# Batch 0 of an attention and GLU kernel: folded norm products, inverses ahead of the score copies, one exp per column block

**Chip, cores, metric.** The kernel runs on one core of one Trainium2 chip. The metric is the device time of one execution in microseconds (us), given as the median of several executions. Experiments 1 and 2 ran on one chip, 3 to 5 on a second and 6 on a third, each with the kernel before beside them (829.74, 829.61 and 829.73 us), so small differences of time are compared only within one of these calls. TensorE does the matrix products, VectorE and ScalarE the work on single elements (the exps and sigmoids on ScalarE), and the DMA engines the loads.

## The reference, cut to what matters

```python
# q, k, v: (4, 6016, 256); tau = 1; w_gate, w_val: (256, 1536); w_out: (1536, 256)
qn = q / (np.linalg.norm(q, axis=1, keepdims=True) + 1e-06)     # a norm per column, over the 6016 rows
kn = k / (np.linalg.norm(k, axis=1, keepdims=True) + 1e-06)
s = kn.transpose(0, 2, 1) @ qn / tau                            # 256 x 256 scores per batch
a = np.exp(s - s.max(-1, keepdims=True))
a /= a.sum(-1, keepdims=True) + 1e-09
x = (v @ a).reshape(24064, 256)
gate = 1.0 / (1.0 + np.exp(-(x @ w_gate)))
return gate * (x @ w_val) @ w_out
```

The scores of a batch need all of its rows of q and k. So batch 0 begins with a stretch in which 12 MB of rows are loaded while TensorE can do no more than follow them. Only then can the dense part (the GLU of all rows) begin. It takes nearly all of the time. While it runs for one batch, the scores of the next are made beside it.

## The kernel before: the parts that matter

The loads stand in one queue, in this order: all q and k rows of batch 0 but the first group, the first rows of v, and the six weight tiles (gate and value in turn).

```python
    for t0, nt in groups0[2:]:
        load_qk(0, t0, nt)
    load_v(0, 0)
    ...
    for fg in range(NFG):
        for w, src in enumerate((moe_w_gate, moe_w_val)):
            nc.gpsimd.dma_start(out=w_sb[w][fg], in_=...)
    load_v(0, 1)
```

The squares of the rows are added up on VectorE. What is not added up goes to TensorE on its own, as "norm products" (a product with a column of ones, `ps_n`). After the last scores follow the norm products, the square root, the inverses, the spreading of the key norms over the partitions (`ps_rk`), and the exps:

```python
    for n, (sq, nt) in enumerate(parts):           # parts: the sum, the eleventh group, two short groups
        norm_mms(ps_n0, sq, nt, n == 0, n == len(parts) - 1, (1, 0) if n else (0, 1))
    st[0]["n"] = ps_n0
    norms_sqrt(0)
    nc.scalar.preload_act_table(ACT.Exp)
    copy_s(0, 0)
    norms_inv(0)
    copy_s(0, 1)
    busy(3)                                        # filler products of no use
    spread_k(0, 0, pso, "o")
    spread_k(0, 1, pso, "o")
    busy(1)
    weights(0, 0)                                  # two multiplications and two exps each
    weights(0, 1)
    ... # transposes of the first v rows
    sums(0, 0)
    gh(0, 0, psg, "g", act=False)
    gh(0, 1, psv, "v", act=True)
    sums(0, 1, pss, "s")
    gh(0, 2, psg, "g", act=False)
    gh(0, 3, psv, "v", act=True)
    nc.scalar.preload_act_table(ACT.Sigmoid)
    gh(0, 4, pso, "o", act=False)
```

`gh` multiplies the 256 x 256 attention weights (`e_sb`) with one tile of a GLU weight. This gives `ps_gh` in a bank of PSUM, the memory that takes TensorE's results, and VectorE or ScalarE evicts it (copies it out) to `gh_G` or `gh_H`. There are twelve such products. I number them from the first: the first needs the first gate weights, the second the first value weights. The fifth and the following share two banks (`pso`), and from the sixth on they stand between the first dense GLU products.

Of the kernel before, what the change touches and what calls it, by code (L numbers as in the profile page):

```python
# [9 lines left out]
FP32 = mybir.dt.float32  # L10
BF16 = mybir.dt.bfloat16
ACT = mybir.ActivationFunctionType
ALU = mybir.AluOpType
# [4 lines left out]
def kernel(  # L18
# [20 lines left out]
    nc = tc.nc  # L39
    P = nc.NUM_PARTITIONS  # L40
# [7 lines left out]
    NT = N // P  # L48
    CB = C // P
# [3 lines left out]
    TPC = 4  # L53
# [12 lines left out]
    def pool(name, bufs, **kw):  # L66
        return ctx.enter_context(tc.tile_pool(name=name, bufs=bufs, **kw))
# [4 lines left out]
    attp = pool("attp", 1)  # L72
# [14 lines left out]
    def mm(out, lhsT, rhs, start, stop, **kw):  # L87
        nc.tensor.matmul(out, lhsT=lhsT, rhs=rhs, start=start, stop=stop, **kw)  # L88
# [21 lines left out]
    t0, nt = groups0[0]  # L110
# [15 lines left out]
    shift = consts.tile([P, 1], FP32)  # L126
# [10 lines left out]
    for fg in range(NFG):  # L137
        for w, src in enumerate((moe_w_gate, moe_w_val)):
            nc.gpsimd.dma_start(
                out=w_sb[w][fg],  # L140
                in_=src.rearrange("(t p) f -> p t f", p=P)[:, :, ds(fg * FG, FG)],
# [11 lines left out]
    def score(b, t0, u):  # L153
        q_sb, k_sb = qk[b, t0]
        if t0 == 0 and u == 0:
            st.setdefault(b, {})["s"] = pss.tile([P, CB, C], FP32, tag="s", name="ps_s")
        ps_s = st[b]["s"]
        t = t0 + u
        for j in range(CB):
            mm(  # L160
                ps_s[:, j, :],
                q_sb[:, u, ds(j * P, P)],
                k_sb[:, u, :],
                start=(t == 0 and j == 0),
                stop=(t == NT - 1),
                skip_group_check=True,
            )

    def squares(b, t0, nt, which, engine, sq=None):
        src = qk[b, t0][which]  # L170
        if sq is None:
            sq = sqpool.tile([P, TPC, C], BF16, tag=f"sq{which}", name=f"sq{which}")
        if engine is nc.scalar:
            nc.scalar.activation(out=sq[:, :nt, :], in_=src[:, :nt, :], func=ACT.Square)  # L174
        else:
            engine.tensor_tensor(  # L176
                out=sq[:, :nt, :], in0=src[:, :nt, :], in1=src[:, :nt, :], op=ALU.mult
            )
        return sq

    def norm_mms(ps, sqs, nt, first, last, order=(0, 1)):

        for w in order:
            sq = sqs[w]
            for u in range(nt):
                for j in range(CB):
                    mm(
                        ps[:, w * CB + j : w * CB + j + 1],
                        sq[:, u, ds(j * P, P)],
                        ones_bf[:, 0:1],  # L190
                        start=(first and w == order[0] and u == 0 and j == 0),
                        stop=(last and u == nt - 1),
                        skip_group_check=True,
                    )

    def acc_start(b):
        st.setdefault(b, {})["acc"] = [
            attp.tile([P, TPC, C], BF16, tag=f"acc{w}", name=f"acc{w}") for w in range(2)
        ]
# [75 lines left out]
    def norms_sqrt(b):  # L275
        s = st[b]
        s["r"] = attp.tile([P, 2 * CB], FP32, tag="r", name="r")
        nc.scalar.activation(out=s["r"], in_=s["n"], func=ACT.Sqrt)

    def norms_inv(b):  # L280
        r = st[b]["r"]
        nc.vector.tensor_scalar(out=r, in0=r, scalar1=1e-6, scalar2=None, op0=ALU.add)
        nc.vector.reciprocal(r, r)
        if inv_tau != 1.0:
            nc.vector.tensor_scalar(
                out=r[:, :CB], in0=r[:, :CB], scalar1=inv_tau, scalar2=None, op0=ALU.mult
            )
# [8 lines left out]
    def copy_s(b, j):  # L296
        s = st[b]
        if j == 0:
            s["x"] = attp.tile([P, CB, C], FP32, tag="x", name="x_sb")
        nc.vector.tensor_copy(out=s["x"][:, j, :], in_=s["s"][:, j, :])  # L300

    def weights(b, i):

        s = st[b]
        e = attp.tile([P, CB, P], BF16, tag=f"e{i}", name=f"e_sb{i}", bufs=2)
        for j in range(CB):
            y = attp.tile([P, P], FP32, tag=f"y{i}{j}", name="y_sb")
            nc.vector.tensor_tensor(
                out=y, in0=s["x"][:, j, ds(i * P, P)], in1=s["rk"][i], op=ALU.mult
            )  # L310
            nc.scalar.activation(  # L311
                out=e[:, j, :], in_=y, func=ACT.Exp, bias=shift, scale=s["r"][:, j : j + 1]
            )
        s.setdefault("e", []).append(e)
        s.setdefault("rrow", [])

# [152 lines left out]
    def busy(n):  # L469

        ps = psg.tile([P, CH], FP32, tag="g", name="ps_busy")
        for _ in range(n):
            mm(ps, ones_bf, ones_wide, True, True)

    ps_n0 = psm.tile([P, 2 * CB], FP32, tag="m", name="ps_n")

    n_acc = NT // TPC - 1
    acc_start(0)
    acc = st[0]["acc"]
    last0 = len(groups0) - 1  # L480
    parts = [(acc, TPC)]
    for g, (t0, nt) in enumerate(groups0):
        engines = (nc.vector, nc.scalar) if g < last0 else (nc.scalar, nc.vector)
        sq = [squares(0, t0, nt, w, engines[w], acc[w] if g == 0 else None) for w in range(2)]
        if 0 < g < n_acc:
            for w in range(2):
                nc.vector.tensor_tensor(out=acc[w], in0=acc[w], in1=sq[w], op=ALU.add)  # L487
        elif g:
            parts.append((sq, nt))
        for u in range(nt):  # L490
            score(0, t0, u)
        if n_acc - 3 <= g <= n_acc:
            busy(1)

    for n, (sq, nt) in enumerate(parts):
        norm_mms(ps_n0, sq, nt, n == 0, n == len(parts) - 1, (1, 0) if n else (0, 1))
    st[0]["n"] = ps_n0
    norms_sqrt(0)
    nc.scalar.preload_act_table(ACT.Exp)
    copy_s(0, 0)  # L500
    norms_inv(0)
    copy_s(0, 1)
    busy(3)
    spread_k(0, 0, pso, "o")
    spread_k(0, 1, pso, "o")
    busy(1)
    weights(0, 0)
    weights(0, 1)
    late = []
    transpose_v(  # L510
# [123 lines left out]
```

## Time and profile before

| before | us |
|---|---|
| median of 3 runs (range) | 829.78 (829.66 to 829.87) |
| span of the profiled execution | 827.8 |
| last key rows landed | 32.86 |
| first / second `ps_gh` | 36.92 / 37.35 |
| eighth `ps_gh` | 42.82 |

The page says that TensorE is busy 98% of the time. That is an average over a start in which it is not the bound and a dense part in which it is. Such a change is read from the start alone: what waits there, and for what. The timeline lists instructions in order of time (start, us, engine, line, operation, output and input, shape, count; in brackets the idle time just before and what ended it). These lines of the kernel before, besides those which the prediction shows, matter later:

```profile
33.52 0.84 PE L88 MATMUL ps_n<-ones_bf,sq 128*128 128x1 bf16 x28
...
39.60 1.28 ACT L521 ACT_TABLE_LOAD   x1
...
42.08 0.69 ACT L377 ACTIVATE gh_H<-ps_gh,rrow 128x512 bf16<-128x512 f32 x1
...
42.14 0.74 DVE L379 TENSOR_SCALAR gh_G<-ps_gh,rrow 128x512 bf16<-128x512 f32 x1
...
42.82 0.59 PE L88 MATMUL ps_gh<-w_val,e_sb 128*128 128x512 bf16 x2
```

The first line is the tail of the norm products, to 34.36. The last three belong together. The eighth `ps_gh` starts 0.05 after ScalarE's eviction ends (42.08 + 0.69 = 42.77), while VectorE's still runs, to 42.88.

### The profile page before, as it was taken

To read this page: it belongs to the slowest core of one execution; us is meant where nothing else is said; L and a number is where in the kernel's file an instruction comes from. 1 tells how busy PE (TensorE), PEld (TensorE's weight loads), DVE (VectorE), ACT (ScalarE), POOL (GpSimd) and SP (SyncE) were. 2 spreads that over 40 slices of the span, in tenths; PEclk is the share of its full clock that TensorE was granted. 3 is DMA by queue.
4 is the path that set the end of the run, shared out by engine and by line. 5 is a ranking of instruction groups with operands and counts; after the bars stand their busy time and mean duration, and the time that the engine had idled before them with its cause. 6 is when DMAs were issued, how large, how long until landed. Compare 5 with 4: busy or idle time off the path is not lost.

```text
span 827.8 us, 13658 instructions
## 1 busy us (share of the span) xinstructions
PE 810.3 (98%) x5138; PEld 500.3 (60%) x5150; DVE 590.4 (71%) x1025; ACT 391.7 (47%) x644; POOL 83.4 (10%) x159
## 2 busy tenths in 40 slices
PE   4899999999999999999999999999999999999998
PEld 3556666665665666665575666666566566666566
DVE  6677877787667777778767777777766666666665
ACT  4654444446644444445654444444655444444442
POOL 5532100002210100000211010000000000000000
PEclk8799999999999999999999999999999999999999
DMA  9999633226746433223876452223322423322111
GB/s 208 207 205 213 108 52 90 58 55 136 159 85 120 97 87 61 55 52 85 156 141 127 81 101 62 51 62 77 64 60 63 73 52 85 69 49 69 47 36 71
DMA packets 79026, 77.17 MB, mean 93 GB/s; under 512 B 50800, under 2 KB 55920, under 8 KB 78960
## 3 DMA queue, kind: packets, MB, share of 16 engines
q0 software_dynamic: 23920, 38.81, 28.3%
q1 hardware_dynamic: 54752, 36.91, 17.5%
q8 instruction: 40, 0.66, 0.3%
q10 hardware_dynamic: 288, 0.59, 0.2%
q14 instruction: 26, 0.21, 0.1%
HBM read 78.64 MB, written 24.64 MB: 125 GB/s over the span
## 4 chain that ended last, share of the span: by engine, by line
PE 95%; DMA 3%; POOL 1%; DVE 1%; issue 0%; ACT 0%; POOLq 0%
PE ps_o L88 30%; PE ps_gate L88 29%; PE ps_val L88 29%; PE ps_s L88 4%; DMA k_sb<-in_k_dram 3%; PE ps_gh L88 2%; DVE hT L424 0%; POOL q_sb L97 0%; PE ps_n L88 0%; POOL k_sb L97 0%; DVE sq L176 0%; PE ps_end L88 0%; ACT g_sb L423 0%; ACT e_sb L311 0%; PE ps_busy L88 0%
## 5 line engine op out<-in xcount | busy, mean ns | idle before, releaser
L424 DVE TENSOR_TENSOR hT<-ps_val,g_sb 128x512 bf16<-128x512 f32 (+1 forms) x576 | 391.2, 680 | 205.2 <-ACT g_sb L423 200.7
L423 ACT ACTIVATE g_sb<-ps_gate 128x512 bf16<-128x512 f32 (+1 forms) x576 | 338.3, 588 | 385.9 <-PE ps_gate L88 379.6
L88 PE MATMUL ps_gate<-vT,gh_G 128*128 128x512 bf16 (+1 forms) x1152 | 337.6, 375 | 0.2
L88 PE MATMUL ps_val<-vT,gh_H 128*128 128x512 bf16 (+1 forms) x1152 | 337.5, 375 | 0.3
L88 PE MATMUL ps_o<-w_out_sb,hT 128*128 128x256 bf16 x2244 | 324.9, 273 | 0.0
L88 PEld LDWEIGHTS <-hT 128*128 128x128 bf16 x2268 | 221.0, 98 | 124.6
L88 PEld LDWEIGHTS <-gh_H 128*128 128x128 bf16 x1152 | 112.7, 98 | 131.6 <-issue 1.0
L88 PEld LDWEIGHTS <-gh_G 128*128 128x128 bf16 x1152 | 112.4, 98 | 37.8 <-DVE gh_G L379 0.5
L106 POOL DMA_DIRECT2D v_sb<-in_v_dram x48 | 25.6, 533 | 620.5 <-DMA vT<-v_sb 487.5
L450 DVE COPY out_sb<-ps_o 128x256 f32<-128x256 f32 x187 | 77.4, 414 | 12.6 <-PE ps_o L88 12.6
L88 PE MATMUL ps_s<-k_sb,q_sb 128*128 128x256 bf16 x376 | 73.1, 298 | 13.2 <-ACT k_sb L130 7.0
L88 PEld LDWEIGHTS <-q_sb 128*128 128x128 bf16 x376 | 40.0, 106 | 23.6 <-issue 8.9
L215 DVE TENSOR_TENSOR acc<-acc,sq 128x1024 bf16<-128x1024 bf16 (+1 forms) x66 | 44.2, 669 | 0.0
L176 DVE TENSOR_TENSOR sq<-q_sb 128x1024 bf16<-128x1024 bf16 (+2 forms) x44 | 29.4, 667 | 0.7 <-DMA q_sb<-in_q_dram 0.7
L97 POOL DMA_DIRECT2D q_sb<-in_q_dram x48 | 26.6, 553 | 14.4 <-DMA q_sb<-in_q_dram 8.6
L97 POOL DMA_DIRECT2D k_sb<-in_k_dram x48 | 26.1, 545 | 16.8 <-DMA k_sb<-in_k_dram 8.4
L176 DVE TENSOR_TENSOR sq<-k_sb 128x1024 bf16<-128x1024 bf16 (+2 forms) x34 | 22.4, 658 | 0.9 <-DMA k_sb<-in_k_dram 0.9
L174 ACT ACTIVATE sq<-k_sb 128x1024 bf16<-128x1024 bf16 (+1 forms) x11 | 11.2, 1018 | 13.7 <-DMA k_sb<-in_k_dram 13.7
L487 DVE TENSOR_TENSOR acc<-acc,sq 128x1024 bf16<-128x1024 bf16 x18 | 12.5, 692 | 5.2 <-ACT sq L174 4.9
L88 PE MATMUL ps_gh<-w_val,e_sb 128*128 128x512 bf16 x45 | 13.6, 379 | 0.2
L88 PEld LDWEIGHTS <-e_sb 128*128 128x128 bf16 x112 | 10.2, 97 | 4.7 <-ACT e_sb L311 0.5
L88 PE MATMUL ps_gh<-w_gate,e_sb 128*128 128x512 bf16 x41 | 12.8, 379 | 0.2
(67 smaller groups left out, 116.6 us busy)
## 6 DMA issues: line engine op xcount, KB each, us to landing
out_dram<-out_sb SPq DMA_DIRECT2D x44, 512.0 KB, 2.9
v_sb<-in_v_dram POOLq DMA_DIRECT2D x44, 256.0 KB, 3.9
q_sb<-in_q_dram POOLq DMA_DIRECT2D x43, 256.0 KB, 7.5
k_sb<-in_k_dram POOLq DMA_DIRECT2D x43, 256.0 KB, 8.3
out_dram<-out_sb SPq DMA_DIRECT2D x3, 384.0 KB, 3.5
w_gate<-in_moe_w_gate_dram POOLq DMA_DIRECT2D x3, 256.0 KB, 7.9
w_val<-in_moe_w_val_dram POOLq DMA_DIRECT2D x3, 256.0 KB, 8.0
w_out_sb<-in_moe_w_out_dram POOLq DMA_DIRECT2D x1, 768.0 KB, 13.2
```

The source lines that it names most:

```text
L88: nc.tensor.matmul(out, lhsT=lhsT, rhs=rhs, start=start, stop=stop, **kw)
L97: nc.gpsimd.dma_start(out=tl[:, :nt, :], in_=rows(src, b)[:, t0 : t0 + nt, :])
L106: nc.gpsimd.dma_start(out=v_sb[:, :nt, :], in_=rows(v, b)[:, t0 : t0 + nt, :])
L174: nc.scalar.activation(out=sq[:, :nt, :], in_=src[:, :nt, :], func=ACT.Square)
L176: engine.tensor_tensor(out=sq[:, :nt, :], in0=src[:, :nt, :], in1=src[:, :nt, :], op=ALU.mult)
L215: nc.vector.tensor_tensor(out=acc[:, :nt, :], in0=acc[:, :nt, :], in1=st[b]["sq", w][:, :nt, :], op=ALU.add)
L423: nc.scalar.activation(out=g_sb[:, :n], in_=ps_gate[:, :n], func=ACT.Sigmoid)
L424: nc.vector.tensor_tensor(out=hts[b, ci][:, f, :n], in0=ps_val[:, :n], in1=g_sb[:, :n], op=ALU.mult)
L450: nc.vector.tensor_copy(out=out_sb[:, s, :], in_=ps)
L487: nc.vector.tensor_tensor(out=acc[w], in0=acc[w], in1=sq[w], op=ALU.add)
```

## The change

The intent is a shorter way from the last key rows to the first exp. The squares of the eleventh four-row group join the sum on VectorE, which held ten groups before, so 16 norm products fall away. The other 28 are issued ahead of the last scores. The inverses stand ahead of both score copies. The column norm moves from the exp's scale into a fused multiplication, so that one exp of 256 columns takes the place of two of 128.

```diff
@@ weights(b, i)
+        y = attp.tile([P, CB, P], FP32, tag=f"y{i}", name="y_sb")
         for j in range(CB):
-            y = attp.tile([P, P], FP32, tag=f"y{i}{j}", name="y_sb")
-            nc.vector.tensor_tensor(out=y, in0=s["x"][:, j, ds(i * P, P)], in1=s["rk"][i], op=ALU.mult)
-            nc.scalar.activation(out=e[:, j, :], in_=y, func=ACT.Exp, bias=shift, scale=s["r"][:, j : j + 1])
+            nc.vector.scalar_tensor_tensor(
+                out=y[:, j, :], in0=s["x"][:, j, ds(i * P, P)], scalar=s["r"][:, j : j + 1],
+                in1=s["rk"][i], op0=ALU.mult, op1=ALU.mult)
+        nc.scalar.activation(out=e, in_=y, func=ACT.Exp, bias=shift)
@@ loop over the row groups of batch 0 (cut)
-    n_acc = NT // TPC - 1
+    n_acc = NT // TPC
...
+        if g == last0:
+            norm_mms(ps_n0, acc, TPC, True, False)
+            for n, (end, rows_n) in enumerate(ends):
+                norm_mms(ps_n0, end, rows_n, False, n == len(ends) - 1, (1, 0) if n else (0, 1))
         for u in range(nt):
             score(0, t0, u)
...
-    for n, (sq, nt) in enumerate(parts):
-        norm_mms(ps_n0, sq, nt, n == 0, n == len(parts) - 1, (1, 0) if n else (0, 1))
     st[0]["n"] = ps_n0
     norms_sqrt(0)
     nc.scalar.preload_act_table(ACT.Exp)
+    norms_inv(0)
     copy_s(0, 0)
-    norms_inv(0)
     copy_s(0, 1)
```

(Some lines of the diff are joined here to save room, and the bookkeeping of the delayed add is cut.)

More of the change, by code (lines that the diff above doesn't have):

```diff
@@ L305, in weights @@
         e = attp.tile([P, CB, P], BF16, tag=f"e{i}", name=f"e_sb{i}", bufs=2)
+        y = attp.tile([P, CB, P], FP32, tag=f"y{i}", name="y_sb")
         for j in range(CB):
-            y = attp.tile([P, P], FP32, tag=f"y{i}{j}", name="y_sb")
-            nc.vector.tensor_tensor(
-                out=y, in0=s["x"][:, j, ds(i * P, P)], in1=s["rk"][i], op=ALU.mult
-            )
-            nc.scalar.activation(
-                out=e[:, j, :], in_=y, func=ACT.Exp, bias=shift, scale=s["r"][:, j : j + 1]
-            )
+            nc.vector.scalar_tensor_tensor(
+                out=y[:, j, :],
+                in0=s["x"][:, j, ds(i * P, P)],
+                scalar=s["r"][:, j : j + 1],
+                in1=s["rk"][i],
+                op0=ALU.mult,
+                op1=ALU.mult,
+            )
+        nc.scalar.activation(out=e, in_=y, func=ACT.Exp, bias=shift)
         s.setdefault("e", []).append(e)
@@ L480 @@
     last0 = len(groups0) - 1
-    parts = [(acc, TPC)]
+    adds, ends = [], []
     for g, (t0, nt) in enumerate(groups0):
@@ L484 @@
         sq = [squares(0, t0, nt, w, engines[w], acc[w] if g == 0 else None) for w in range(2)]
+        while adds:
+            w, last_sq = adds.pop()
+            nc.vector.tensor_tensor(out=acc[w], in0=acc[w], in1=last_sq, op=ALU.add)
         if 0 < g < n_acc:
-            for w in range(2):
-                nc.vector.tensor_tensor(out=acc[w], in0=acc[w], in1=sq[w], op=ALU.add)
-        elif g:
-            parts.append((sq, nt))
+            nc.vector.tensor_tensor(out=acc[0], in0=acc[0], in1=sq[0], op=ALU.add)
+            if g < n_acc - 1:
+                nc.vector.tensor_tensor(out=acc[1], in0=acc[1], in1=sq[1], op=ALU.add)
+            else:
+                adds.append((1, sq[1]))
+        elif g:
+            ends.append((sq, nt))
+        if g == last0:
+            norm_mms(ps_n0, acc, TPC, True, False)
+            for n, (end, rows_n) in enumerate(ends):
+                norm_mms(ps_n0, end, rows_n, False, n == len(ends) - 1, (1, 0) if n else (0, 1))
         for u in range(nt):
             score(0, t0, u)
-        if n_acc - 3 <= g <= n_acc:
+        if n_acc - 4 <= g < n_acc:
             busy(1)
-    for n, (sq, nt) in enumerate(parts):
-        norm_mms(ps_n0, sq, nt, n == 0, n == len(parts) - 1, (1, 0) if n else (0, 1))
     st[0]["n"] = ps_n0
```

## The prediction

> **What bounds the kernel now.** I read the page's busy shares first, then the engines' busy time by stretches, then the chain of work that ended last around the start of batch 0, then the timeline of the same stretch, and last the issue-to-landing times of the weights.
>
> ```profile
> PE 810.3 (98%) x5138; PEld 500.3 (60%) x5150; DVE 590.4 (71%) x1025; ACT 391.7 (47%) x644; POOL 83.4 (10%) x159
> ...
> 6.50:28.00 21.50, 15.82 (x73) 10.31 (x75) 16.88 (x26) 9.95 (x10) 9.60 (x19) 0.72 1.12 209
> 28.00:33.30 5.30, 4.32 (x32) 2.81 (x31) 3.03 (x6) 3.05 (x4) 3.56 (x6) 0.83 1.19 204
> 35.00:39.00 4.00, 3.67 (x28) 2.21 (x28) 3.22 (x12) 3.69 (x8) 1.63 (x3) 1.00 1.24 203
> 54.00:90.00 36.00, 36.00 (x234) 22.64 (x232) 26.45 (x45) 15.37 (x26) 9.68 (x19) 1.00 1.04 193
> ```
>
> TensorE (first engine in each row) is busy 98% of the span, and from 54 us on without a gap. The change touches only batch 0, of which everything lies before 38 us, so what can be won is only an earlier start of the dense part. The last columns show another thing: the DMA engines are full (share above 1) and move a steady 203 to 209 GB/s until well past 39 us.
>
> ```profile
> 26.38 6.48 DMA k_sb<-in_k_dram
> ...
> 32.91 0.38 PE ps_s L88 x2
> 33.28 1.08 PE ps_n L88 x44
> ...
> 35.13 0.47 PE ps_rk L88 x2
> ...
> 35.63 0.30 DVE y_sb L308
> ...
> 35.95 0.89 ACT e_sb L311 x2
> ...
> 37.06 0.88 PE ps_gh L88 x4
> ```
>
> This is the chain (start, us, what). The last key rows land at 26.38 + 6.48 = 32.86. Then come the last scores, 44 norm products, square root and inverse, the spreading of the key norms (ps_rk), a multiplication, two exps, and the first weight products (ps_gh). From 32.86 to the first ps_gh at 36.92 are 4.06 us: this is the stretch that the change shortens.
>
> ```profile
> 28.67 0.71 POOL L139 DMA_DIRECT2D w_gate<-in_moe_w_gate_dram  x1 [0.70 <-DMA k_sb<-in_k_dram]
> 29.89 0.72 POOL L139 DMA_DIRECT2D w_val<-in_moe_w_val_dram  x1 [0.52 <-DMA q_sb<-in_q_dram]
> ...
> 36.92 0.59 PE L88 MATMUL ps_gh<-w_gate,e_sb 128*128 128x512 bf16 x2
> ...
> 37.35 0.59 PE L88 MATMUL ps_gh<-w_val,e_sb 128*128 128x512 bf16 x2
> ...
> w_gate<-in_moe_w_gate_dram POOLq DMA_DIRECT2D x1, 256.0 KB, 7.9
> ...
> w_val<-in_moe_w_val_dram POOLq DMA_DIRECT2D x1, 256.0 KB, 7.3
> ```
>
> The last two lines are the issues of just these two transfers, with us to landing. So the first gate weights land at 28.67 + 7.9 = 36.57 and the first value weights at 29.89 + 7.3 = 37.19 (the landing records in the trace say 36.54 and 37.23). They are used at 36.92 and 37.35. **The slack is 0.35 and 0.12 us**, and of it the signal takes about 0.05 (keys: landed 32.86, used 32.91). The weights are not on the chain, but stand right behind it.
>
> **What the Trainium skill says.** (1) "ScalarE: Activation LUTs", section "What ACT_TABLE_LOAD costs": an ACTIVATE with a bias pointer takes about 280 ns + 0.833 ns per element, a further pointer operand adds about 93 ns, and neighbours overlap by about 93. Estimate from it: two exps of 128 columns with two pointers 2 x 479 - 93 = 865 ns, one of 256 with one pointer 493 ns. The trace agrees: 0.89 us for the pair in the chain, and 500 ns for the wide form, which later batches use. (2) "VectorE: DVE Perf Modes", "The perf-mode tier table (the rule you actually need)": tensor_tensor on fp32, or with any PSUM operand, runs at one element per cycle, so the fused form gains no speed there. It has no row for scalar_tensor_tensor. In the trace that costs some 60 ns more at the same size (474 ns at 256 columns against 415 for a tensor_tensor of 256). (3) "SBUF — State Buffer", "Who interferes with whom": a VectorE op with two SBUF inputs contends with GpSimd's reads, and the page infers that descriptor generation, done by GpSimd, needs the write side. So two more adds should not delay the weight issues beside them. The trace fits: issues of q and k take 0.53 us all through the stretch full of such adds.
>
> ```profile
> L266 DVE SCALAR_TENSOR_TENSOR x_sb<-ps_s,n_sb 128x256 f32<-128x256 f32 x6 | 2.6, 474 | 0.0
> L308 DVE TENSOR_TENSOR y_sb<-x_sb,ps_rk 128x128 f32<-128x128 f32 x4 | 0.9, 282 | 0.3 <-PE ps_rk L88 0.3
> L321 ACT ACTIVATE e_sb<-x_sb,shift 128x256 bf16<-128x256 f32 x6 | 2.7, 500 | 0.7 <-DVE x_sb L266 0.7
> L311 ACT ACTIVATE e_sb<-y_sb,shift,r 128x128 bf16<-128x128 f32 x4 | 1.6, 482 | 0.1
> ```
>
> **The change part by part.**
> *Squares of the eleventh group.* Two VectorE adds of 128x1024 bf16 more (692 ns each, by the group of L487), 16 norm products fewer (44 to 28; 28 of them stood in 0.77 us of weight loads, so 27 ns each: 0.44 us). The adds fit into gaps. The first runs 30.89 to 31.58, and the next square began at 31.59 anyway. The second waits for ScalarE's square (30.95 + 1.06 = 32.01), runs 32.08 to 32.77, and the last square cannot start before 32.96. Cost on the chain: none.
> *Norm products ahead of the last scores.* They can begin after the scores of the group before (about 32.7), and only the last four need the last squares, which end at 33.25. They end about 33.56 instead of 34.36: **0.80 us** earlier.
> *Inverses in one pass.* The code already computed all four in one pair of small ops. The pair (0.17 + 0.18 us) now stands ahead of both copies. Square root at 33.6, inverse done 34.19. The two copies (0.4 us each, overlapping to 0.75) end at about 34.85. TensorE, after the scores and three filler products, can spread the norms at about 34.4 (three fillers of 0.22 after 33.75), not 35.13. ps_rk took 0.50 until y could start, so y starts about 34.93 against 35.63: **0.70 us** earlier. The exp table load, 1.28 us from 33.8, is done at 35.1 and hidden.
> *Weights.* Before: one multiplication (0.30) and then two exps (to 36.84), 1.21 us after 35.63. After: two fused multiplications, about 0.25 + 0.34 by my estimate from 474 ns less 128 elements, then one exp of 0.50: 1.12 us with hand-overs. So **0.09 us** more. The first exp block is ready at about 36.05 instead of 36.84: 0.79 us in all.
> *What remains of it.* The first ps_gh may start at 36.1, but its weights are there only at 36.54 + 0.05 = 36.59: 0.33 earlier than 36.92. The next two need 37.23 + 0.05 = 37.28 against 37.35: **0.07 us**. From there TensorE runs back to back to the third weight tile (landed 38.51, used 38.63). ScalarE's chain, which loads the sigmoid table after the second H tile (table load at 39.60, first sigmoid 40.90, then hT, then the eviction that frees the bank of a ps_gh at 42.82), hangs on these products and moves by the same 0.07. VectorE's first evictions may come 0.28 earlier and take away a small stall at 39.3, but the ps_gh at 42.82 waits for the ScalarE chain again. Sum: 0.07 us of 829.78 gives **829.7 us**.
>
> **The rivals.** *The whole gain survives* (0.8 us, so 829.0). It needs the weights to land some 0.7 us earlier. For it: nothing in the change's way stops the transfers. Against: they are paced by earlier landings and a full DMA at 205 GB/s, and no added or moved instruction frees one. *Half survives* (0.3 us, so 829.5), if the earlier VectorE evictions carry through and the later wait at 42.8 is looser than I read it, or if the value weights land a little earlier in other executions. *The change costs time* (0.2 to 0.5 us, so 830.0 to 830.3), if the late add holds the last square, or if the fused multiplication is much slower with a PSUM operand. Against: 0.19 us of room before the last square, and 0.45 us of room ahead of the gate weights. *The clock*: it is at half speed from 16 to 29.8 us in this trace. "TensorE: Matmul & The Clock Gate", "Part 1: The HAM clock gate (the "warmup" mystery)", ties it to free-running windows of about 3.4 us. The clock column shows the half (0.72 and 0.83 in the mixed stretches, 1.00 after). The fillers keep their places, so I expect no change but some scatter.
>
> **Range and chances.** All paths lie between a saving of 0.8 and a loss of 0.5 us, which is 0.1% either way. The three runs of before spread over 0.2 us. I take 829.2 to 830.1. A 2% change is 16.6 us, and no path leads there: faster 0.005, same 0.985, slower 0.01.
>
> **What would show it.** In the profile after: 28 ps_n products ending near 33.5; y near 34.9; wide exps ending near 36.1; then TensorE idle some 0.5 us until the first ps_gh at about 36.6, with that wait put down to the w_gate transfer; the first value products near 37.3; and the first dense glu products shifted by 0.05 to 0.3 us only. I am wrong if the weights land more than 0.2 us from 36.54 and 37.23, if the first exp ends later than 36.5, or if the time falls by more than 0.5 us.

## The result and the profile after

The changed kernel takes 829.91 us (median of 6 runs, 829.73 to 830.0). The kernel before took 829.79 in the same rounds (6 runs, 829.66 to 829.94). The ratio is 1.0001, with a 95% interval from 0.9988 to 1.0014: the same. All ratios here are the mean time of one kernel's runs over that of the other's of the same rounds, so they are not quite the ratio of the medians that I quote.

The page's busy times, and the windows (us, then busy time with instruction count of PE, PEld, DVE, ACT and POOL, then granted clock, DMA share, GB/s) of the kernel after:

```profile
PE 807.7 (98%) x5134; PEld 498.5 (60%) x5134; DVE 591.7 (71%) x1027; ACT 391.1 (47%) x642; POOL 83.1 (10%) x159
```

```profile
28.00:33.30 5.30, 3.79 (x52) 2.98 (x52) 4.14 (x8) 3.05 (x4) 3.83 (x6) 1.00 1.18 204
35.00:39.00 4.00, 2.82 (x22) 1.33 (x20) 2.87 (x10) 2.25 (x5) 1.36 (x3) 1.00 1.24 204
```

In the second window TensorE does 2.82 us of work where it did 3.67, although nothing of the weight products has fallen away. Work moved to an earlier time, and a hole opened. The DMA rate is 204 GB/s (203 before). The clock column of the first window (1.00, before 0.83) is scatter between executions: a repeat of the kernel before showed 1.00 there, and a repeat of the kernel after 0.84.

The timeline of the kernel after:

```profile
32.84 0.44 PE L88 MATMUL ps_n<-ones_bf,sq 128*128 128x1 bf16 x12
...
34.56 1.12 DVE L308 SCALAR_TENSOR_TENSOR y_sb<-x_sb,r,ps_rk 128x128 f32<-128x128 f32 x4
...
36.38 0.60 PE L88 MATMUL ps_gh<-w_gate,e_sb 128*128 128x512 bf16 x2 [0.42 <-DMA w_gate<-in_moe_w_gate_dram]
...
37.39 0.59 PE L88 MATMUL ps_gh<-w_val,e_sb 128*128 128x512 bf16 x2 [0.41 <-DMA w_val<-in_moe_w_val_dram]
...
41.95 0.69 ACT L380 ACTIVATE gh_H<-ps_gh,rrow 128x512 bf16<-128x512 f32 x1
...
42.17 0.74 DVE L382 TENSOR_SCALAR gh_G<-ps_gh,rrow 128x512 bf16<-128x512 f32 x1
...
42.96 0.59 PE L88 MATMUL ps_gh<-w_val,e_sb 128*128 128x512 bf16 x2
```

The multiplications begin at 34.56, where they began at 35.63. The two brackets are the point: TensorE now waits 0.42 us for the gate weights and 0.41 for the value weights. The second product starts at 37.39, and it started at 37.35 before. A gain of 0.8 us goes in (1.07 less the 0.25 by which the last keys landed earlier), and nothing comes out. The last three lines show something else. The eighth product now starts 0.05 after **VectorE's** eviction (42.17 + 0.74 = 42.91), while ScalarE's ended long before, at 42.64.

The chain of work that ended last, around this stretch (start, us, what):

```profile
29.64 7.71 DMA w_val<-in_moe_w_val_dram
...
37.39 0.59 PE ps_gh L88 x2
...
38.93 0.69 ACT gh_H L380
...
39.63 1.28 ACT L531
...
42.17 0.75 DVE gh_G L382
...
42.96 0.59 PE ps_gh L88 x2
```

Before, the chain came from the key rows through norms, `ps_rk`, y and exps. Now it comes from the transfer of the value weights. None of the work that the change shortens is on it any more. Between 37.39 and 42.96 it runs through the second H eviction, the table load for the sigmoid (L531) and an eviction on VectorE.

**Where the end is set.** From the eighth `ps_gh` on, every kernel runs the same way. Its span less the start of this product is 785.0 us, within 0.1, in all fourteen profiles (before 827.8 - 42.82 = 784.98, after 828.0 - 42.96 = 785.04). So a profile can be judged by this one start.

### The profile page after: what moved, and what is told of

It is laid out like the page before. It is cut to its first block, busy times and chain, and to the rows that moved or that the text cites. A ratio compares the mean times of both kernels' runs of the same rounds, so it can differ in the third digit from the quotient of the medians. Undisturbed runs are those within 1.5% of the kernel's fastest.

```text
span 828.0 us, 13639 instructions
## 1 busy us (share of the span) xinstructions
PE 807.7 (98%) x5134; PEld 498.5 (60%) x5134; DVE 591.7 (71%) x1027; ACT 391.1 (47%) x642; POOL 83.1 (10%) x159
## 4 chain that ended last, share of the span: by engine, by line
PE 94%; DMA 4%; DVE 1%; ACT 0%; issue 0%; POOL 0%; POOLq 0%
PE ps_o L88 30%; PE ps_val L88 29%; PE ps_gate L88 29%; PE ps_s L88 4%; DMA q_sb<-in_q_dram 3%; PE ps_gh L88 2%; DMA w_val<-in_moe_w_val_dram 1%; DVE hT L427 0%; ACT g_sb L426 0%; DVE sq L176 0%; PE ps_end L88 0%; ACT L531 0%; PE ps_n L88 0%; DVE gh_G L382 0%; ACT gh_H L380 0%
## 5 line engine op out<-in xcount | busy, mean ns | idle before, releaser
L88 PE MATMUL ps_s<-k_sb,q_sb 128*128 128x256 bf16 x376 | 70.4, 288 | 15.6 <-DMA k_sb<-in_k_dram 8.7
L380 ACT ACTIVATE gh_G<-ps_gh,rrow 128x512 bf16<-128x512 f32 x13 | 8.9, 687 | 8.1 <-PE ps_gh L88 6.4
```

The costliest lines, as they stand in the source:

```text
L88: nc.tensor.matmul(out, lhsT=lhsT, rhs=rhs, start=start, stop=stop, **kw)
L380: nc.scalar.activation(out=dst, in_=ps, func=ACT.Copy, scale=r)
```

## The experiments

The theory (A): the change does what it intends, and the gain is lost in the wait for weights that land no earlier. The rival (B): the gain is small in itself or is given back further on, by slower multiplications or by the evictions.

### 1. The weights a transfer earlier, in both kernels

The first v rows are not loaded, and a tile that is there is taken in their place. The result is wrong on purpose. With 256 KB less ahead of them, the weights come earlier by one transfer.

```diff
-    load_v(0, 0)
+    vs[0, 0] = qk[0, 0][0]
```

On the kernel before:

> The kernel before, without the load of the first v tile (its place is taken by a q tile that is there already, so the result is wrong on purpose). One transfer of 256 KB less stands ahead of the gate and value weights, so these land about 1.25 us earlier; one landing follows the other by that much. Theory A (the weights' arrival hides the change): in the kernel before the weights were not what was waited for, so the time stays within 0.3 us of 829.8. Rival B (the change saves nothing because the added VectorE work gives it back): the same here.

On the kernel after:

> The changed kernel, without the load of the first v tile (wrong on purpose). Theory A: the first product with the gate weights now starts when the exps are ready, some 3.2 us after the last keys instead of 3.8, and the first with the value weights 0.9 us or more earlier than in the changed kernel; the time is 0.7 to 1.0 us under that of the kernel before without the same load, so about 829.0. Rival B: no difference between the two, both about 829.8.

Measured in the same rounds: before_nov0 829.57 (ratio to the kernel before 0.9999), after_nov0 829.00 (0.9993, interval 0.9977 to 1.001). The difference of the medians is 0.57 us, and 0.48 by the means (829.59 and 829.11). It has the sign that A expects, and somewhat less than its size. The chains say why. First before_nov0:

```profile
35.77 0.89 ACT e_sb L311 x2
...
36.88 0.89 PE ps_gh L88 x4
```

Then after_nov0:

```profile
28.52 7.98 DMA w_val<-in_moe_w_val_dram
...
36.54 0.59 PE ps_gh L88 x2
```

Without the v load the kernel before still hangs on its exps. The kernel after hangs on the value weights again, which landed at 28.52 + 7.98 = 36.50. But that is not what makes the gain smaller than expected. At the seventh `ps_gh` it is 0.79 us (41.27 and 40.48, in the table of experiment 3), and at the eighth 0.51 (42.63 and 42.12). Experiment 3 shows what is lost between the two.

### 2. The weights a transfer later, in both kernels

The second v load is moved up ahead of the weights. Both kernels stay correct.

```diff
     load_v(0, 0)
+    load_v(0, 1)
...
-    load_v(0, 1)
     nc.gpsimd.dma_start(out=w_out_sb, ...)
```

> The kernel before, with the load of the second v tile moved ahead of the weights (correct result): all weights land about 1.25 us later. Theory A: the value weights become the wait in this kernel too; their slack was about 0.1 us, so the time grows by 1.0 to 1.3 us to about 830.9. Rival B: the chain of norms and exps sets the start, and the growth is under 0.5 us.

> The changed kernel with the second v tile's load ahead of the weights (correct result). Theory A: the wait for the weights grows by 1.25 us and nothing of the change can be seen any more: within 0.3 us of the kernel before with the same edit, about 831.0. Rival B (the change itself costs what it saves in the chain): also equal to it, but both within 0.5 us of 829.8.

Measured: before_wlate 831.01, after_wlate 830.94, both at a ratio of 1.0019 to the kernel before (one run of each was at 832.4, which the record does not explain). The kernel before had 829.74 in these rounds: the growth of 1.27 us is the one that A expects, and B expects less than 0.5. The first weight product in the timeline of before_wlate:

```profile
37.18 0.60 PE L88 MATMUL ps_gh<-w_gate,e_sb 128*128 128x512 bf16 x2 [0.31 <-DMA w_gate<-in_moe_w_gate_dram]
```

The same in after_wlate:

```profile
37.19 0.61 PE L88 MATMUL ps_gh<-w_gate,e_sb 128*128 128x512 bf16 x2 [1.07 <-DMA w_gate<-in_moe_w_gate_dram]
```

The starts agree within 0.01 us. The wait for the transfer has grown from 0.31 to 1.07 us: the 0.76 us that the change saves turns into waiting one for one. Where the weights are late enough, the change is worth nothing. This is what A says, and B has no reason for it. (At the eighth product after_wlate is even 0.25 us later, 44.04 and 43.79, which the medians do not show; experiment 3 tells why.)

### 3. The two parts of the change, each alone

Both without the first v load, so both are wrong. nov0_norms has the new norm section and the old `weights()`. nov0_exps has the old norm section and the new `weights()`.

```diff
 nov0_norms, against after_nov0           nov0_exps, against before_nov0
-  weights(): fused, one wide exp         -  weights(): two tensor_tensor, two exps
+  weights(): as before                   +  weights(): fused, one wide exp
```

> Part alone: the squares, the norm products and the inverses as in the changed kernel, the weights' multiplication and exps as before; the first v tile not loaded (wrong on purpose), so that the weights come early. My sum says that this part carries nearly all of the shortening of the chain: y starts 1.95 us after the last keys land (2.8 before), the first exp block is ready 3.15 us after them (4.0 before). The time is then within 0.15 us of the changed kernel without that load, 829.0 to 829.2. Rival: the fused multiplication and the wide exp carry a real share, then it stays above 829.3.

> The other part alone: only the fused multiplication and one exp per column block, norms as before, the first v tile not loaded (wrong on purpose). My sum: the first exp block about 0.1 us earlier after y starts (1.12 instead of 1.21 us), so the time is 0 to 0.15 us under the 829.57 us of the kernel before without that load. Rival: this part carries a real share, then 829.3 or less.

Measured in the same rounds: nov0_norms 828.79 (ratio 0.9989), nov0_exps 829.83 (1.0004). I had expected the second to come out at or just under 829.57, the time of before_nov0 in the rounds of experiment 1: a miss. The first came out 0.2 below its range, which was 829.0 to 829.2. Two lines of the timeline of nov0_norms:

```profile
36.11 0.59 PE L88 MATMUL ps_gh<-w_gate,e_sb 128*128 128x512 bf16 x2
...
41.26 0.69 ACT L377 ACTIVATE gh_H<-ps_gh,rrow 128x512 bf16<-128x512 f32 x1
```

And of nov0_exps:

```profile
36.67 0.59 PE L88 MATMUL ps_gh<-w_gate,e_sb 128*128 128x512 bf16 x2
...
41.88 0.74 DVE L382 TENSOR_SCALAR gh_G<-ps_gh,rrow 128x512 bf16<-128x512 f32 x1
```

The last keys do not land at the same time in each execution, so the start of the first `ps_gh` is counted from there. In before_nov0 the two are 36.74 - 32.63 = 4.11 us apart, in nov0_norms 36.11 - 32.84 = 3.27, in nov0_exps 36.67 - 32.59 = 4.08, in after_nov0 35.90 - 32.68 = 3.22. So the norm section is worth 0.84 to 0.86 us and the wide exp 0.03 to 0.05 us.

The second lines tell why nov0_exps is no faster in the end. In nov0_norms the eighth product starts at 42.00, behind ScalarE's eviction (41.26 + 0.69 = 41.95). It cannot have waited for VectorE's, which ran until 42.10. In nov0_exps it starts at 42.68, behind VectorE's (41.88 + 0.74 = 42.62). The table of the starts shows this for all kernels whose order of work on ScalarE is otherwise the same (before_again and after_again are repeats of the two kernels):

| kernel | `weights()` | seventh `ps_gh` | eighth | step |
|---|---|---|---|---|
| before | old | 41.45 | 42.82 | 1.37 |
| before_again | old | 41.39 | 42.76 | 1.37 |
| before_nov0 | old | 41.27 | 42.63 | 1.36 |
| before_wlate | old | 42.38 | 43.79 | 1.41 |
| nov0_norms | old | 40.63 | 42.00 | 1.37 |
| after | new | 41.32 | 42.96 | 1.64 |
| after_again | new | 41.33 | 42.98 | 1.65 |
| after_nov0 | new | 40.48 | 42.12 | 1.64 |
| after_wlate | new | 42.40 | 44.04 | 1.64 |
| after_pad (experiment 6) | new | 41.43 | 43.07 | 1.64 |
| nov0_exps | new | 41.20 | 42.68 | 1.48 |

Nothing but `weights()` differs between nov0_norms and after_nov0, and the step grows from 1.37 to 1.64. So this **0.27 us comes with the new `weights()`**. Counted from the last keys, the eighth product starts 10.00 us after them in before_nov0, 9.16 in nov0_norms, 9.44 in after_nov0 and 10.09 in nov0_exps. With early weights the norm section thus brings its 0.84 us to the dense part in full, and the new `weights()` takes 0.28 of it back. In the instruction order of the built programs the eighth product of the kernel before waits for ScalarE, that of the kernel after for VectorE:

```
before  Matmult ps_gh<-w_val,e_sb 128x512 [waits Activation_49]
after   Matmult ps_gh<-w_val,e_sb 128x512 [waits DVE_49]
```

(The names in brackets are the semaphores that ScalarE and VectorE raise.) The reason is in the built programs too. In all fourteen the sixth product lies in PSUM bank 5 and the seventh in bank 4. The eighth lies in bank 4 with the old `weights()`, and so waits for ScalarE's eviction of the seventh. With the new one it lies in bank 5, and waits for VectorE's eviction of the sixth. Why the builder hands out the other bank is not shown.

### 4. The weights ahead of v, in a correct kernel

If the weights are what is late, the first v rows could come behind the first two weight tiles.

```diff
-    load_v(0, 0)
...
+        if fg == 0:
+            load_v(0, 0)
...
-    transpose_v(0, 0, ...)         # from ahead of the first gh
-    nc.scalar.copy(*late.pop())
...
     gh(0, 3, psv, "v", act=True)
+    transpose_v(0, 0, ...)
+    nc.scalar.copy(*late.pop())
```

> The changed kernel with the first gate and value weights ahead of the first v tile in the queue and the v transposes behind the fourth weight product (correct result). If the weights' arrival is what holds it, the first gate product starts as soon as the exps are ready, 3.2 us after the last keys, the first value product about 0.9 us earlier than in the changed kernel, and the time falls by 0.3 to 0.6 us to about 829.4; the v tile then becomes the next wait, as it lands where the value weights landed. If not, the time stays at 829.9 or grows, as the transposes now stand on the path.

Measured: 830.12 (ratio 1.0005). The hoped-for gain is a miss, and the stated alternative came true. Two lines of the timeline of after_v0late:

```profile
36.62 0.59 PE L88 MATMUL ps_gh<-w_val,e_sb 128*128 128x512 bf16 x2 [0.16 <-DMA w_val<-in_moe_w_val_dram]
...
39.73 0.59 PE L88 MATMUL ps_gate<-vT,gh_G 128*128 128x512 bf16 x2 [0.26 <-ACT vT L531]
```

The second product starts at 36.62, which is 0.77 us earlier than in the kernel after. But then the first dense product waits for the transposed v rows, whose two copies now stand behind the weight products. It starts at 39.73, and the eighth `ps_gh` at 43.18 in place of 42.96. A wait has been exchanged for another, a longer one.

### 5. The sigmoid's table load in the hole

The chain after runs through the second H eviction and a table load of 1.28 us. ScalarE, however, is idle before that: it waits 1.33 us for its first eviction. So I moved the load there. The kernel stays correct.

```diff
     nc.scalar.copy(*late.pop())
+    nc.scalar.preload_act_table(ACT.Sigmoid)
     gh_tiles(0)
...
     gh(0, 3, psv, "v", act=True)
-    nc.scalar.preload_act_table(ACT.Sigmoid)
```

> The changed kernel with the sigmoid table loaded ahead of the first two H evictions on ScalarE, in the 1.3 us in which that engine now waits for the value weights (correct result). In the changed kernel the chain from the value weights on runs through the second H eviction, the table load (1.28 us), the first sigmoid, hT and the eviction that frees a bank, and TensorE stands still for some 0.4 us in all between 41.8 and 43 us. If that chain is what holds, the stalls go and the time falls by 0.3 to 0.45 us to about 829.5. If TensorE is bound by the weights alone, the time stays at 829.9.

Measured: 829.37 (ratio to the kernel before of the same rounds 0.9997). The timeline of after_table:

```profile
36.74 1.28 ACT L524 ACT_TABLE_LOAD   x1
...
42.38 0.59 PE L88 MATMUL ps_gh<-w_val,e_sb 128*128 128x512 bf16 x2
```

The load runs in the hole, from 36.74 to 38.02. The eighth product starts at 42.38, and its step behind the seventh (41.08) is 1.30. That is what TensorE needs for the three pairs of products from one to the next, at 0.43 us a pair as the chain of the dense part has them: the wait for a bank is gone. That is 0.34 of the 0.58 us by which the eighth product comes earlier than in the kernel after. The other 0.24 is scatter: the value weights landed at 37.11 in this execution, and at 37.35 in the other. A repeat followed, beside the kernel after itself.

### 6. Repeats, and the packet on one DMA engine

The landings of a transfer are on record for each of the 16 DMA engines, though without the engine's number. They show that one engine is late. In the kernel before, 15 engines had delivered the first gate weights by 35.43, and the last one came at 36.55. In the kernel after these are 35.17 and 36.33, and for the value weights 36.42 and 37.35. In both, a packet of 16 KB of kind "instruction" runs on one engine for 0.94 us shortly before, at 34.2 to 34.5. To see whose it is, after_pad issues 64 small products of no use behind the scores of groups 1 to 8. They fall into a stretch in which TensorE waits for rows, so they should cost nothing, but TensorE has gone through 128 more instructions (a weight load each) by then.

```diff
         for u in range(nt):
             score(0, t0, u)
+        if 1 <= g <= 8:
+            ps = psg.tile([P, CH], FP32, tag="g", name="ps_pad")
+            for _ in range(8):
+                mm(ps[:, :1], ones_bf, ones_bf[:, 0:1], True, True)
```

The other three runs are repeats, two of them in five rounds, to measure the small differences on one chip: after_again (the kernel after), before_again (the kernel before) and after_table_again (experiment 5).

> The changed kernel once more, for more rounds and a second profile. Theory A: the first value product starts when the value weights have landed on the last of the 16 engines, at 37.1 to 37.5 us, whatever the exps do; time within 0.2 us of the kernel before. If the 0.1 us by which it was slower is only where the last engine stood in that one execution, the difference from before comes out between -0.15 and +0.15 us this time; if the change itself delays the weights, it is +0.1 or more again and the value weights land later than in the second profile of before.

> The kernel before once more, for a second profile. Expected: first gate product about 4.06 us after the last keys land, first value product right behind it, gate weights landing at 36.3 to 36.6 and value weights at 37.1 to 37.5; ratio to itself 1.000.

> The changed kernel with the sigmoid table loaded ahead of the two H evictions, on the same chip as the changed kernel this time (correct result). If the chain of table load, sigmoid, hT and eviction behind the value weights is what used up the rest of the gain: 0.3 to 0.5 us under the changed kernel and under the kernel before, about 829.4, with no stall of TensorE between 37.2 and 45 us. If it was scatter of the other call: no difference.

> The changed kernel with 64 products of one column each (and as many weight loads) more on TensorE in the early groups, where it waits for data anyway (correct result). In every profile so far one 16 KB instruction packet is moved at 34.2 to 34.5 us, and from then on one of the 16 DMA engines lands its share 0.6 to 1.2 us behind the others. If the packet is TensorE's program, fetched as it is used up, it moves to some 28 to 31 us with 128 instructions more ahead of it, and the last engine falls behind there: the last keys land late instead and the time stays within 0.3 us. If it is not TensorE's, it stays at 34.2 to 34.5 us.

| run | median (range), us | ratio to before | 95% interval |
|---|---|---|---|
| before_again | 829.76 (829.71 to 829.82) | 1.0001 | 0.9987 to 1.0015 |
| after_again | 829.91 (829.75 to 830.3) | 1.0003 | 0.9991 to 1.0016 |
| after_table_again | 829.56 (829.37 to 829.75) | 0.9999 | 0.9986 to 1.0011 |
| after_pad | 829.93 (829.78 to 830.14) | 1.0002 | 0.9987 to 1.0018 |

The kernel after is again slower than the kernel before, by 0.15 to 0.18 us in the medians and 0.19 to 0.26 in the means. The profiles of these two repeats agree: their eighth products start at 42.98 and 42.76, 0.22 apart. The interval of the ratio holds 1, so the sign rests on two sets of rounds and the profiles, not on one ratio. By the letter of what I had written for after_again, this says that the change delays the weights. The value weights did land later: at 37.35 and 37.36 in the two profiles after, at 37.23 and 37.09 in the two before. Whether the change causes that, no run tests. It is not what costs the time, as the seventh products come no later (41.32 and 41.33, before 41.45 and 41.39). With the table load moved, the kernel is 0.40 us faster than the kernel after by the means (829.55 and 829.95), and 0.14 faster than the kernel before. It is the best correct kernel, by an amount that counts as the same. I had expected 0.3 to 0.5 under both: right against the kernel after, a miss against the kernel before.

In after_pad the packet came at 21.78. The DMA view of the stretch from 21.5 to 23 (packets, MB, share) has it:

```profile
q8 instruction: 1, 0.02, 3.9%
```

In the stretch from 33.5 to 35 there is none any more; the next comes at 41.20. It moved further than the 28 to 31 us that I expected. But TensorE's instructions are all that was changed, so I take it for a part of TensorE's program. From then on it is the key rows too that are complete 0.95 us later than on 15 engines (32.69 and 33.64), and the gate weights come at 36.20 (15 engines at 35.28). The total time did not move. In the other profiles one engine comes 1.06 to 1.32 us late in the first transfer that lands after the packet, and 0.46 to 1.10 us late in the weights that follow. It does not stay late for ever: in after_nov0 the last engine is only 0.06 us behind in the transfer that lands at 46.27. What sets these sizes is open.

## Why the prediction was right, step by step

The number was right (829.7 predicted, 829.91 measured, in the range), and so was its main argument: the weights end the gain. Experiments 1 to 3 show it from both sides: with late weights the change is worth nothing, and with early ones the norm section brings its whole 0.84 us. A part of the rival B holds as well: 0.27 us is given back at the evictions. So the sign of what remains was wrong, and that the number still fit is owed to the smallness of all these effects: the range of 829.2 to 830.1 holds a saving as well as a loss. Not all terms of the sum had the right size. Since the keys landed 0.25 us earlier in the profile after (32.61, before 32.86), I count from there where it matters.

- **Squares of the eleventh group.** Right. The adds cost nothing on the chain: the last square on VectorE waited for the key rows, and ran as soon as they were there.
- **Norm products ahead of the last scores.** Right. 28 products end at 33.28, predicted 33.56, so in the same place counted from the keys.
- **Inverses in one pass.** Right in kind, a little undersized. y starts 1.95 us behind the keys, predicted 2.07, before 2.77: 0.82 gained where I had 0.70. Experiment 3 gives 0.84 for this part by its own run.
- **Weights.** The step's sum was close. From the start of y to the end of the first exp block it took 1.15 us, predicted 1.12, before 1.21. The four fused multiplications start every 0.26 us, the four of before every 0.20. The two wide exps take 1.02 us where four narrow ones took 1.65, but only the first is on the path. At the first weight product the step gives 0.03 to 0.05, not 0.09.
- **What remains.** Here was the step that failed: "the ps_gh at 42.82 waits for the ScalarE chain again". The second product came at 37.39, predicted about 37.3, before 37.35. The keys and gate weights of this execution were 0.2 us early, the value weights 0.12 late. TensorE's sequence was even 0.13 us ahead at the seventh product (41.32, before 41.45), as the small stall at 39.3 fell away, which the prediction had as possible: the first pair of `ps_gate` took 0.76 us before and takes 0.59. (The fifth product, which uses the third weight tile, starts at 38.70 in the profile before, not at 38.63 as the prediction reads; nothing hangs on it.) But the eighth waited for VectorE's eviction of the sixth, not for the ScalarE chain, and this cost 0.27. So a predicted gain of 0.07 became a loss of 0.14 in the profiles (42.96 against 42.82). I had read the wait at 42.82 from the profile of before and taken it over. The order of the instructions of the changed kernel would have shown that the wait had changed its engine.
- **The slack.** The 0.35 us that I allowed the gate weights were real, but I had them as paced by a full DMA. For 15 of 16 engines these weights were there at 35.4, ahead of the first exp of either kernel. The last engine, by the times the one that carried an instruction packet, made them 1.1 us later. That does not change what the change is worth, only the reason. One of the prediction's own signs of being wrong came true by a hair: the gate weights landed at 36.33, 0.21 us from 36.54.

**The rivals.** That the whole gain survives was out: it would have needed weights 0.7 us earlier. Even with a whole transfer taken away the gain of the whole change was 0.5 to 0.6 us, though the norm section alone then kept its 0.84. That half survives did not happen either: the value weights did not land earlier, and the wait at 42.8 was not looser. That the change costs time is what happened, at the low edge of its size (0.1 to 0.26 us), but by neither of the ways that I gave it: the late add did not hold the last square, and the slower fused multiplication did not reach the end. The clock played no part that can be seen: from 35 to 39 us the granted clock was 1.00 in both profiles.

## What to carry to other kernels

Before a chain is shortened, look at what arrives next to it: the gain at that point can be no larger than the distance to the next landing. Here 0.9 us were saved and the distance was 0.35 and 0.12. When a wait of the old kernel is taken over into an estimate, check in the changed program's order that it still waits for the same engine. The kernel that this suggests, the new norm section with the old `weights()` in a correct form, was not run. And a hole that a change opens can be worth more than the change, if something later on the chain, here a table load, can be moved into it.

## What the Trainium skill lacked or had wrong

- "VectorE: DVE Perf Modes", "The perf-mode tier table (the rule you actually need)", has no row for scalar_tensor_tensor. At 128x128 in fp32 with one PSUM operand, four back to back took 1.12 us (a start every 0.26), four tensor_tensor of the same size 0.88 (a start every 0.20).
- "Runtime: NRT & Kernel Launch", section "Instruction fetch mechanics", says that a sequencer fetches its program in blocks of 16 KiB and that crossing a boundary is "mostly hidden". The size agrees with the packet seen here. It is not hidden for the data beside it: the packet takes one of 16 DMA engines for 0.94 us, and the last engine's share of the weights that landed after it came 0.46 to 1.32 us behind the others.
- "DMA: Bandwidth & Descriptors", section "Why a DMA increments its semaphore by 16 and not by 1", says that only the full count means that all data has landed. The runs agree, and the page could add the cost: the gate weights stood at 15 of 16 at 35.17 and were complete at 36.33 in the kernel after.
- "ScalarE: Activation LUTs", section "What ACT_TABLE_LOAD costs", gives 1283 ns for the load and about 1380 ns of drain besides. The load is 1.28 us in every profile here. The drain is not seen: in the kernel after the load starts at 39.63, just behind the eviction before it (38.93 + 0.69 = 39.62), it ends at 39.63 + 1.28 = 40.91, and the first sigmoid starts at 40.93.
